# One column group for the final sum of a decode step: four shifted weight windows, one cast, one store of eight rows

## The chip, the cores and the metric

The kernel runs on one core of a Trainium2 chip. The metric is the device time of one execution in microseconds (us), the median of several runs. All times below are in us unless ns is written. The engines are named as in the profile: PE is TensorE (PEld its weight loads), DVE is VectorE, ACT is ScalarE, POOL is GpSimd, SP is SyncE, whose queue starts nearly all transfers.

## The reference

Two batch rows (`B = 2`, one token each, `D = 512`) go through an attention block with cached keys and values and, beside it, through a small dense block; a gate mixes the two results.

```python
g = sigmoid((x * gate_w).sum(-1, keepdims=True))
q = x @ wq                                  # 512 -> 32 heads x 128
p = softmax(q . k_cache / sqrt(128))        # 32 heads, 4096 cached positions, per batch row
a = (p . v_cache) @ wo                      # 4096 -> 512
b = relu(x @ w1) @ w2                       # 512 -> 1376 -> 512
out = g * a + (1 - g) * b                   # (2, 1, 512), bf16
```

The caches are 2 x 64 MB in bf16, wq and wo 4 MB each, w1 and w2 1.4 MB each. All inputs are bf16.

## The kernel before

**Order of the work.** Each engine has a list of instructions written out by hand; a small helper (`_Prog`) turns named markers into semaphore waits. SP's queue loads wq and w1, then ten pieces of the key cache and eleven of the value cache into a few regions of one SBUF tile `kv`, each as soon as its region has been read (line 286), then a part of w2 (`w2x`, line 289), wo in two parts (semaphores `wo0`, `wo1`, lines 291 and 293; wo's rows 0 to 23 and 24 to 31) and the rest of w2 in three parts of 7, 2 and 1 rows (`w2b`, `w2c`, `w2d`, line 295). Here a "row" of wo or w2 is one contraction step: 128 partitions x 512 columns. The last entry of the queue is the store of the result (line 296).

**Start.** GpSimd fills constants (lines 232 to 260), among them `ident16`, from which VectorE makes the selection matrices `selx` and `sel2` (lines 324 and 326). TensorE computes the gate, q (lines 344 and 424) and turns q by transposes (line 371); the dense block's hidden row is made, and `ffn_relu` writes it, with relu and the factor `1 - g`, into `hT` (line 406): `[128, 14, 2]`, that is 14 contraction rows of two weight columns, one for each batch row.

**Middle.** VectorE transposes key tiles (line 417), TensorE computes scores (line 445, with a second matmul on held weights, line 424, through the helper `mm_held`), then softmax, then the values in four column groups at a time (line 510). Line 537 gathers head results with fp32 matmuls into one column group.

**The tail.** After the last value piece `o_turn` (line 549) turns the attention result into `oW` (line 552): `[128, 32, 2]`, 32 contraction rows of two weight columns. The output is a sum over 32 rows of wo and 14 of w2. `project` (line 564) handles the four `w2x` rows and wo's rows 0 to 23 with matmuls of 512 columns, row r in column group r % 4, so that four partial sums stand at PSUM partitions 0, 32, 64 and 96. VectorE copies them to SBUF as `pr_sb` (line 569). `last_rows` then runs `fin_row` (line 573) for wo's rows 24 to 31, for `pr_sb` with `sel2` as weights (this adds the four partial sums), and for ten rows of w2. In `fin_row` the 512 output columns are cut into four pieces of 128; piece c is computed in column group c and lands on partitions 32c and 32c + 1:

```python
for c in range(4):
    e.matmul(psf(32 * c, 32 * c + 2, FIN_C0, 128), lhsT=lhsT, rhs=rhs[:, c * 128:(c + 1) * 128],
             tile_position=(0, 32 * c))
```

`store` casts two pieces on VectorE (line 592) and two on ScalarE (line 594) into `out_sb`, `[2, 512]`, and SP stores it as two rows of 1024 bytes.

Of the kernel before, what the change touches and what calls it, by code (L numbers as in the profile page):

```python
# [14 lines left out]
HALF = 16384  # L15
REGION = {"A": 0, "Ah": HALF, "B": 2 * HALF, "C": 4 * HALF}
WO_CUT = 24


class _Marker:  # L20
# [67 lines left out]
def bass_gated_mix__gqa_block_cached__dense_activation_relu__decode_kernel(  # L88
# [50 lines left out]
    nrow = sb("nrow", [128, 8, 4], dt.float32)  # L139
    negm = sb("negm", [128, 32], dt.float32)  # L140
    lsum = sb("lsum", [128, 2, 2], dt.float32)
    sel2 = sb("sel2", [128, 2], dt.float32)
    lrow = sb("lrow", [128, 2], dt.float32)
    rinv = sb("rinv", [32, 2], dt.float32)
    mask8 = sb("mask8", [128, 8], dt.bfloat16)
# [3 lines left out]
    sell_odd = sell[:, 1:65].rearrange("p (u f two) -> p u f two", u=8, two=2)[:, :, :, 0]  # L149
    s4 = sb("s4", [32, 4, 128], dt.bfloat16)  # L150
    O_sb = sb("O_sb", [32, 2, 128], dt.bfloat16)
    oW = sb("oW", [128, 32, 2], dt.bfloat16)
    hT = sb("hT", [128, 14, 2], dt.bfloat16)
    out_sb = sb("out_sb", [2, 512], dt.bfloat16)
    w2x = sb("w2x", [128, 4, 512], dt.bfloat16)
    hrowT = kt[:, 2, 0:448]

# [35 lines left out]
        return m  # L193


    both, lo, hi = (0, 1), (0,), (1,)
    k_pieces = [(0, both, "A"), (1, both, "B"), (2, lo, "C"), (3, both, "A"), (4, both, "B"), (2, hi, "C"),
                (5, both, "A"), (6, both, "B"), (7, lo, "C"), (7, hi, "A")]
# [21 lines left out]
    def pool(fn, waits=(), signal=None):  # L220
        P.add("pool", fn, waits=[marker(w) for w in waits], signal=marker(signal) if signal else None)
# [7 lines left out]
    def pe(fn, waits=(), signal=None, dwaits=()):  # L229
# [4 lines left out]
    pool(lambda g: g.affine_select(out=ident16[:], in_=ident16[:], pattern=[[-1, 128]],  # L234
                                   compare_op=ALU.not_equal, fill=1.0, base=0, channel_multiplier=1),
         waits=["c_i16z"], signal="c_i16")
    pool(lambda g: g.memset(xTw[:], 0.0), signal="c_xTw")
    pool(lambda g: g.memset(qbuf[:], 0.0), signal="c_qbuf")  # L238
    pool(lambda g: g.memset(mpad[:], 0.0), signal="c_mpad")
    pool(lambda g: g.memset(w2x[:], 0.0), signal="c_w2x")  # L240
    pool(lambda g: g.memset(sell[:], 0.0), signal="c_s0")  # L241
    pool(lambda g: g.memset(sell_odd, 1.0), waits=["c_s0"], signal="c_s1")
# [50 lines left out]
    sp(lambda e: e.dma_start(wreg[:, 512 * WO_CUT:HALF], wo_in[:, 512 * WO_CUT:HALF]).then_inc(sem["wo1"], 16))  # L293
    for name, r0, r1 in (("w2b", 0, 7), ("w2c", 7, 9), ("w2d", 9, 10)):
        sp(lambda e, name=name, r0=r0, r1=r1: e.dma_start(w2[:, r0:r1, :], w2_in[:, r0:r1, :]).then_inc(sem[name], 16))
    sp(lambda e: e.dma_start(out.rearrange("b s n -> (b s) n"), out_sb[:, :]).then_inc(sem["out"], 16),
       dwaits=[(sem["fin"], 4)])
    sp(lambda e: e.wait_ge(sem["out"], 16))


    def gate():
        for t in range(4):
            pe(lambda e, t=t: e.transpose(PSB[0:128, XT_B0 + 4 * t:XT_B0 + 4 * t + 3], x_sb[0:3, t::4], ident16[0:3, 0:3]),  # L303
               waits=(["c_i16"] if t == 0 else []), dwaits=([(sem["x"], 16), (sem["gw"], 16)] if t == 0 else []),
               signal=("pe_xT" if t == 3 else None))
        dve(lambda v: v.tensor_copy(out=xT3[:, :, 0:3], in_=PSB[0:128, XT_B0:XT_B0 + 16].rearrange("p (t b) -> p t b", t=4)[:, :, 0:3]),  # L306
            waits=["pe_xT"], signal="dve_xT")
        dve(lambda v: v.tensor_copy(out=xTw[:, :, 0:2], in_=xT), waits=["dve_xT", "c_xTw"], signal="dve_xTw")
        dve(lambda v: v.tensor_tensor(out=xg[:], in0=xT, in1=xT3[:, :, 2:3].to_broadcast([128, 4, 2]), op=ALU.mult),
            waits=["dve_xT"], signal="dve_xg")  # L310
        dve(lambda v: v.tensor_reduce(out=xgs[:], in_=xg[:].rearrange("p t b -> p b t"), axis=AX.X, op=ALU.add),
            waits=["dve_xg"], signal="dve_xgs")
        pe(lambda e: e.matmul(psf(0, 128, G_C0, 2), lhsT=ones32[:, :], rhs=xgs[:, :], start=True, stop=True),
           waits=["dve_xgs", "c_ones"], signal="pe_z")
        act(lambda a: a.activation(out=ez[:], in_=psf(0, 128, G_C0, 2), func=ACT.Exp, scale=-1.0),
            waits=["pe_z"], signal="act_ez")
        dve(lambda v: v.tensor_scalar(out=ez1[:], in0=ez[:], scalar1=1.0, scalar2=None, op0=ALU.add),
            waits=["act_ez"], signal="dve_ez1")
        dve(lambda v: v.reciprocal(out=gb[:], in_=ez1[:]), waits=["dve_ez1"], signal="dve_g")
        dve(lambda v: v.tensor_scalar(out=gm[:], in0=gb[:], scalar1=-1.0, scalar2=1.0, op0=ALU.mult, op1=ALU.add),  # L320
            waits=["dve_g"], signal="dve_gm")
        dve(lambda v: v.tensor_reduce(out=maskc[:], in_=ident16[:].rearrange("p (k c) -> p c k", c=4), axis=AX.X, op=ALU.add),
            waits=["c_i16"], signal="dve_maskc")
        dve(lambda v: v.tensor_reduce(out=selx[:, 24:32], in_=ident16[:].rearrange("p (t h c) -> p h t c", t=4, c=4),
                                      axis=AX.XY, op=ALU.add), waits=["c_i16", "c_selx"], signal="dve_selx")
        dve(lambda v: v.tensor_reduce(out=sel2[:], in_=ident16[:].rearrange("p (t q) -> p q t", t=4)[:, 0:2, :], axis=AX.X, op=ALU.add),
            waits=["c_i16"], signal="dve_sel2")

    def q_window(b, blk, par, u):
        h = 2 * (blk % 2) + par  # L330
# [72 lines left out]
    def ffn_relu():  # L403
        dve(lambda v: v.transpose(out=hrowT, in_=psf(0, 128, HR_C0, 448)), waits=["pe_h"], signal="dve_hrT")
        for b in range(2):
            dve(lambda v, b=b: v.tensor_scalar(out=hT[:, :, b], in0=hrowT[:, b:448:32], scalar1=0.0,
                                               scalar2=gm[:, b:b + 1], op0=ALU.max, op1=ALU.mult),
                waits=["dve_hrT", "dve_gm"], signal=f"dve_h{b + 1}")


    def k_turn(i):
# [6 lines left out]
            waits=([f"pe_sc_{i - NKT}"] if i >= NKT else ["dve_h2"] if i == 2 else []), dwaits=([landed["k", n]] if first else []),  # L418
            signal=(f"k_read_{n}" if turn_end[n] == i else f"kt_{i}"))

    def mm_held(e, out, lhsT, rhs, start, stop, size=(128, 128), at=(0, 0)):
        a = e.lower_ap(rhs)
        w = e.lower_ap(lhsT, for_matmul_weights=True)
        return e.add_instruction(mybir.InstMatmult(  # L424
            start_tensor_calc=start, stop_tensor_calc=stop, tile_size=size, tile_position=at, ldweights=False,
            name=nc.get_next_instruction_name(), engine=mybir.EngineType.PE, ins=[a, w], outs=[e.lower_ap(out)]))

    def k_scores(i):
# [118 lines left out]
    def o_turn():  # L547
        for dq in range(4):
            pe(lambda e, dq=dq: e.matmul(psf(0, 128, R_C0, 64), lhsT=s4[:, dq, :], rhs=O_sb[:, :, 32 * dq:32 * dq + 32],
                                         start=(dq == 0), stop=(dq == 3), tile_position=(0, 0)),  # L550
               waits=(["dve_O0", "dve_O1", "c_s4"] if dq == 0 else []), signal=("pe_R" if dq == 3 else None))
        dve(lambda v: v.tensor_copy(out=oW[:, :, :].rearrange("p r b -> p b r"), in_=psf(0, 128, R_C0, 64).rearrange("p (b r) -> p b r", b=2)),
            waits=["pe_R"], signal="dve_oW")

    def pr_clear():
        dve(lambda v: v.memset(psf(0, 128, PR_C0, 512), 0.0), waits=["act_exp3"], signal="dve_pr0")
# [1 line left out]
    def project(rows):  # L558
        for r in rows:
            t = r % 4  # L560
            lhsT, rhs = (hT[:, 14 + r, :], w2x[:, t, :]) if r < 0 else (oW[:, r, :], wreg[:, r * 512:(r + 1) * 512])
            dw = {-4: [(sem["w2x"], 32)], 0: [(sem["wo0"], 16)]}.get(r, [])
            waits = {-4: ["dve_h2", "dve_pr0"], 0: ["dve_oW"]}.get(r, [])
            pe(lambda e, t=t, r=r, lhsT=lhsT, rhs=rhs: e.matmul(psf(32 * t, 32 * t + 2, PR_C0, 512), lhsT=lhsT, rhs=rhs,
                                                               start=(r < 0), stop=(r >= WO_CUT - 4), tile_position=(0, 32 * t)),
               dwaits=dw, waits=waits, signal=("pe_pr" if r == WO_CUT - 1 else None))

# [1 line left out]
        dve(lambda v: v.tensor_copy(out=pr_sb, in_=psf(0, 128, PR_C0, 512)), waits=["pe_pr"], signal="dve_pr")  # L569

    def fin_row(first, last, lhsT, rhs, dw, waits, signal):
        for c in range(4):
            pe(lambda e, c=c: e.matmul(psf(32 * c, 32 * c + 2, FIN_C0, 128), lhsT=lhsT, rhs=rhs[:, c * 128:(c + 1) * 128],  # L573
                                       start=first, stop=last, tile_position=(0, 32 * c), skip_group_check=True),
               dwaits=(dw if c == 0 else []), waits=(waits if c == 0 else []), signal=(signal if c == 3 else None))

    def last_rows():
        for r in range(WO_CUT, 32):
# [1 line left out]
        fin_row(False, False, sel2[:, :], pr_sb, [], ["dve_pr", "dve_sel2"], None)  # L580
        for r in range(10):
            dw = {0: [(sem["w2b"], 16)], 7: [(sem["w2c"], 16)], 9: [(sem["w2d"], 16)]}.get(r, [])
            fin_row(False, r == 9, hT[:, r, :], w2[:, r, :], dw, [], "pe_fin" if r == 9 else None)

    def store():
        def piece(c):
            return out_sb[:, 128 * c:128 * c + 128], psf(32 * c, 32 * c + 2, FIN_C0, 128)

        for c in range(4):
            dst, src = piece(c)  # L590
            if c < 2:
                dve(lambda v, dst=dst, src=src: v.tensor_copy(out=dst, in_=src).then_inc(sem["fin"], 1), waits=["pe_fin"])
            else:
                act(lambda a, dst=dst, src=src: a.activation(out=dst, in_=src, func=ACT.Copy).then_inc(sem["fin"], 1), waits=["pe_fin"])  # L594


    gate()
# [64 lines left out]
```

## Time and profile before

| what | value |
|---|---|
| time, median of 3 runs (range) | 344.44 (344.37 to 344.48) |
| the profiled execution's own time | 344.36 |
| its span, from the first to the last instruction | 343.0 |
| mean granted TensorE clock, share of full | 0.806 |
| busy: PE / PEld / DVE / ACT / POOL | 199.7 / 52.2 / 192.9 / 15.0 / 9.5 |
| moved from memory | 145.57 MB, mean 424 GB/s |

The granted clock is the share of its pulses that TensorE's throttle lets through; the views by windows and by slices show it over time. In a view of the timeline, each line is a group of like instructions: start, time that they cover, engine, line of the kernel, operation, tile written <- tiles read, shapes, count, and in brackets the engine's idle time before it with what ended it. In the chain of waits each line is a piece of the chain of work that ended last, in order of time.

### The profile page before, as it was taken

How to read it: one execution, taken by the hardware profiler on the slowest of the kernel's cores; microseconds unless marked ns; L12 is line 12 of the kernel's file. 1: busy time of each engine (PE TensorE's matmuls, PEld its weight loads, DVE VectorE, ACT ScalarE, POOL GpSimd, SP SyncE). 2: the span in 40 equal slices, each digit the busy share in tenths (PEclk: the TensorE clock that was granted, in tenths of full speed). 3: DMA queues.
4: the chain of work that ended last, by engine and by line, in shares of the span. 5: the costliest groups of instructions: out<-in, count | busy, mean ns of one | idle time of the engine just before them, and what ended most of it. 6: DMA issues, size and time to landing. Idle time of an engine off the chain costs nothing.

```text
span 343.0 us, 2484 instructions
## 1 busy us (share of the span) xinstructions
PE 199.7 (58%) x1232; PEld 52.2 (15%) x952; DVE 192.9 (56%) x136; ACT 15.0 (4%) x54; POOL 9.5 (3%) x21
## 2 busy tenths in 40 slices
PE   0440596998797996988999274005065043143656
PEld 0110121111111111111111031002023011021312
DVE  0240896996998996989999596304016103031221
ACT  1040001010001001000000300000000000000000
POOL 8200000000000000000000000000000000000000
PEclk9995599899898999999999767558568656587656
DMA  7998989999999989999999999999999999999996
GB/s 306 470 489 367 489 367 426 432 482 413 443 428 426 485 383 466 390 417 430 428 428 478 436 407 482 405 459 407 405 428 461 420 443 436 397 434 436 419 418 243
DMA packets 4081, 145.57 MB, mean 424 GB/s; under 512 B 459, under 2 KB 592, under 8 KB 872
## 3 DMA queue, kind: packets, MB, share of 16 engines
q1 hardware_dynamic: 4066, 145.43, 98.5%
q8 instruction: 8, 0.13, 0.2%
q14 instruction: 1, 0.01, 0.0%
q10 hardware_dynamic: 6, 0.00, 0.0%
HBM read 145.43 MB, written 0.00 MB: 424 GB/s over the span
## 4 chain that ended last, share of the span: by engine, by line
DMA 65%; PE 17%; DVE 15%; ACT 1%; SPq 0%; issue 0%; DVEq 0%
DMA kv<-in_A_k_cache_dram 27%; DMA kv<-in_A_v_cache_dram 26%; DVE kt L417 12%; DMA kv<-in_B_w_dram 8%; PE PS L510 5%; PE PS L424 5%; PE PS L445 5%; DMA kv<-in_A_wq_dram 4%; PE PS L344 1%; DVE kt L492 1%; ACT kt L465 1%; DVE qrow L368 1%; DVE mpad L453 1%; DVE kt L469 0%; PE PS L371 0%
## 5 line engine op out<-in xcount | busy, mean ns | idle before, releaser
L417 DVE STREAM_TRANSPOSE kt<-kv 128x2048 f32<-128x2048 f32 x64 | 141.1, 2273 | 23.0 <-DMA kv<-in_A_k_cache_dram 23.0
L445 PE MATMUL PS<-kt,qbuf 128*128 128x512 bf16 x256 | 106.1, 414 | 32.8 <-DVE kt L417 27.8
L424 PE MATMUL PS<-kt,qbuf 128*128 128x512 bf16 x256 | 105.5, 412 | 0.0
L510 PE MATMUL PS<-kv,kt 128*32 128x512 bf16 x512 | 46.1, 534 | 90.0 <-DMA kv<-in_A_v_cache_dram 77.1
L518 DVE TENSOR_TENSOR qbuf<-PS,maskc 128x512 f32<-128x512 f32 x11 | 7.6, 692 | 95.8 <-PE PS L510 95.7
L445 PEld LDWEIGHTS PS<-kt,qbuf 128*128 128x128 bf16 x256 | 25.6, 100 | 141.7 <-DVE kt L417 72.8
L510 PEld LDWEIGHTS PS<-kv,kt 128*32 128x32 bf16 x512 | 17.7, 125 | 116.8 <-issue 74.8
L492 DVE TENSOR_TENSOR kt<-kt,mask 128x512 bf16<-128x512 bf16 (+1 forms) x17 | 19.3, 1179 | 0.0
L339 ACT ACTIVATE qbuf<-PS 32x4 bf16<-32x4 bf16 (+1 forms) x40 | 7.6, 190 | 107.9 <-PE PS L424 105.9
L521 DVE TENSOR_REDUCE qbuf<-qbuf 128x128 f32<-128x512 f32 x11 | 11.3, 1025 | 0.4
L344 PE MATMUL PS<-kv,xTw 128*32 128x512 bf16 (+1 forms) x32 | 5.3, 690 | 3.3 <-DMA kv<-in_A_wq_dram 3.3
L594 ACT ACTIVATE out_sb<-PS 2x128 bf16<-2x128 f32 x2 | 0.5, 271 | 144.6 <-PE PS L573 144.6
L537 PE MATMUL PS<-qbuf,selx 128*32 128x128 f32 x22 | 4.9, 387 | 2.0 <-DVE qbuf L521 2.0
L368 DVE CAST qrow<-PS 128x256 bf16<-128x256 f32 x2 | 2.6, 1516 | 5.5 <-PE PS L424 5.5
L465 ACT ACTIVATE kt<-PS,negm 128x512 bf16<-128x512 f32 x4 | 2.7, 686 | 58.9 <-DVE negm L461 58.9
L303 PE MATMUL PS<-ident,x_sb 3*128 3x3 bf16 x4 | 0.3, 166 | 8.1 <-POOL sell L241 8.1
L306 DVE COPY xT<-PS 128x12 bf16<-128x12 bf16 x1 | 0.2, 170 | 8.4 <-PE PS L303 8.4
L238 POOL MEMSET qbuf<- 128x5120 bf16 x1 | 4.4, 4361 | 0.0
L537 PEld LDWEIGHTS PS<-qbuf,selx 128*32 128x32 f32 x22 | 3.4, 162 | 4.6 <-DVE qbuf L521 3.2
L424 PE MATMUL PS<-kv,xTw 128*32 128x512 bf16 (+1 forms) x24 | 3.7, 511 | 0.0
L453 DVE TENSOR_REDUCE mpad<-PS 128x2 f32<-128x2048 f32 x1 | 2.3, 2291 | 2.2 <-PE PS L424 2.2
L469 DVE STREAM_TRANSPOSE kt<-kt 128x1024 bf16<-128x1024 bf16 x2 | 2.5, 1246 | 1.6 <-ACT kt L465 1.5
(67 smaller groups left out, 32.3 us busy)
## 6 DMA issues: line engine op xcount, KB each, us to landing
kv<-in_A_v_cache_dram SPq DMA_DIRECT2D x6, 4096.0 KB, 36.9
kv<-in_A_k_cache_dram SPq DMA_DIRECT2D x4, 4096.0 KB, 31.7
kv<-in_A_wq_dram SPq DMA_DIRECT2D x1, 4096.0 KB, 12.2
kv<-in_A_wo_dram SPq DMA_DIRECT2D x1, 3072.0 KB, 23.4
kv<-in_B_w_dram SPq DMA_DIRECT2D x1, 1376.0 KB, 15.1
kv<-in_A_wo_dram SPq DMA_DIRECT2D x1, 1024.0 KB, 25.5
kv<-in_B_w_dram SPq DMA_DIRECT2D x1, 896.0 KB, 27.2
kv<-in_B_w_dram SPq DMA_DIRECT2D x1, 256.0 KB, 27.4
```

The lines of the kernel that those rows point to most:

```text
L339: act(lambda a: a.activation(out=out, in_=src, func=ACT.Copy), waits=waits, signal=f"q_{b}_{u}_{blk}_{par}")
L344: return e.matmul(out, lhsT=xTw[:, t, :], rhs=rhs, start=(t == 0), stop=(t == 3), tile_position=(0, 32 * c))
L368: dve(lambda v, dst=dst, src=src: v.tensor_copy(out=dst, in_=src), waits=[f"pe_qr{half}"], signal=f"qrow{half}{e2}")
L417: dve(lambda v: v.transpose(out=dst, in_=pairs[:, h, 64 * a:64 * a + 64, :]), waits=([f"pe_sc_{i - NKT}"] if i >= NKT else ["dve_h2"] if i ...
L424: return e.add_instruction(mybir.InstMatmult(start_tensor_calc=start, stop_tensor_calc=stop, tile_size=size, tile_position=at, ldweights=F ...
L445: return e.matmul(out, lhsT=lhsT, rhs=rhs, start=start, stop=stop)
L465: act(lambda a, g=g, par=par: a.activation(out=E_sb[:, 32 * g:32 * g + 32, 16 * par:16 * par + 16], in_=psf(0, 128, (2 * par + g) * BANK, ...
L492: dve(lambda v: v.tensor_tensor(out=out, in0=src.unsqueeze(2).to_broadcast(shape), in1=mask8[:].unsqueeze(1).unsqueeze(3).to_broadcast(sha ...
L510: pe(lambda e, j=j, t=t: e.matmul(psf(32 * t, 32 * t + 32, V_BS[n % 2] * BANK, 512), lhsT=v_weights(n)[:, j], rhs=rows[:, :, j, :], start= ...
L518: dve(lambda e: e.tensor_tensor(out=parts, in0=psf(0, 128, V_BS[n % 2] * BANK, 512).rearrange("p (c d) -> p c d", c=4), in1=maskc[:].unsqu ...
L521: dve(lambda e: e.tensor_reduce(out=X2[:, b, k, :], in_=parts.rearrange("p c d -> p d c"), axis=AX.X, op=ALU.add), waits=[f"dve_m{n}"], si ...
L537: pe(lambda e, n=n, w0=w0: e.matmul(psf(0, 32, O_C0, 128), lhsT=selx[:, w0:w0 + 32], rhs=X2[:, b, n - mine[0], :], start=(n == mine[0]), s ...
```

## The change

All four pieces of 128 output columns are computed in column group 0. The weights of a row become a window of eight columns: `hT`, `oW` and `sel2` are widened from 2 to 11 columns, filled with zeros by GpSimd, and the two batch columns stand at 3 and 7 (`BOTH`). For piece k the window starts at column 3 - k, so that the two real columns stand at k and 4 + k, and the other six are zeros. The four matmuls of a row add into the same eight PSUM partitions; partition 4b + k ends up with piece k of batch row b. One cast on VectorE and one store of eight rows of 128 elements follow. For w2's last row, `held_row` loads a block of 32 weight columns ahead of the wait for `w2d`, and the first of the row's four matmuls runs on it without a load of its own; the other three are ordinary matmuls. Constants: `NB = 4`, `NG = 1`, `WIDE = 11`.

```diff
-    sel2 = sb("sel2", [128, 2], dt.float32)
+    sel2 = sb("sel2", [128, WIDE], dt.float32)
...
-    oW = sb("oW", [128, 32, 2], dt.bfloat16)
-    hT = sb("hT", [128, 14, 2], dt.bfloat16)
-    out_sb = sb("out_sb", [2, 512], dt.bfloat16)
+    oW = sb("oW", [128, 32, WIDE], dt.bfloat16)
+    hT = sb("hT", [128, 18, WIDE], dt.bfloat16)
+    out_sb = sb("out_sb", [32 * NG, 128], dt.bfloat16)
...
+    BOTH = slice(NB - 1, 2 * NB, NB)
...
+    pool(lambda g: g.memset(sel2[:], 0.0), signal="c_sel2")
     pool(lambda g: g.memset(xTw[:], 0.0), signal="c_xTw")
     pool(lambda g: g.memset(qbuf[:], 0.0), signal="c_qbuf")
     pool(lambda g: g.memset(mpad[:], 0.0), signal="c_mpad")
+    pool(lambda g: g.memset(hT[:], 0.0), signal="c_hT")
+    pool(lambda g: g.memset(oW[:], 0.0), signal="c_oW")
     pool(lambda g: g.memset(w2x[:], 0.0), signal="c_w2x")
...
-    sp(lambda e: e.dma_start(out.rearrange("b s n -> (b s) n"), out_sb[:, :]).then_inc(sem["out"], 16),
-       dwaits=[(sem["fin"], 4)])
+    sp(lambda e: e.dma_start(out.rearrange("b s (k n) -> (b s k) n", k=4), out_sb[0:8, :]).then_inc(sem["out"], 16),
+       dwaits=[(sem["fin"], 1)])
...
     def fin_row(first, last, lhsT, rhs, dw, waits, signal):
-        for c in range(4):
-            pe(lambda e, c=c: e.matmul(psf(32 * c, 32 * c + 2, FIN_C0, 128), lhsT=lhsT, rhs=rhs[:, c * 128:(c + 1) * 128],
-                                       start=first, stop=last, tile_position=(0, 32 * c), skip_group_check=True),
+        for n in range(4):
+            k, g = divmod(n, NG)
+            pe(lambda e, k=k, g=g: e.matmul(psf(32 * g, 32 * g + 2 * NB, FIN_C0, 128), lhsT=lhsT[:, NB - 1 - k:3 * NB - 1 - k],
+                                            rhs=rhs[:, (NB * g + k) * 128:(NB * g + k + 1) * 128], start=(first and k == 0),
+                                            stop=(last and k == NB - 1), tile_position=(0, 32 * g), skip_group_check=True),
...
+    def held_row(dw):
+        for g in range(NG):
+            pe(lambda e, g=g: e.ldweights(hT_cols(9 * WIDE + NB - 1), tile_position=(0, 32 * g)))
+        for n in range(4):
+            k, g = divmod(n, NG)
+
+            def fn(e, k=k, g=g):
+                out, rhs = psf(32 * g, 32 * g + 2 * NB, FIN_C0, 128), w2[:, 9, (NB * g + k) * 128:(NB * g + k + 1) * 128]
+                lhsT = hT[:, 9, NB - 1 - k:3 * NB - 1 - k]
+                if k == 0:
+                    return mm_held(e, psf(32 * g, 32 * g + 32, FIN_C0, 128), hT_cols(9 * WIDE + NB - 1), rhs, False, False, (128, 32), (0, 32 * g), True)
+                return e.matmul(out, lhsT=lhsT, rhs=rhs, start=False, stop=(k == NB - 1), tile_position=(0, 32 * g), skip_group_check=True)
+            pe(fn, dwaits=(dw if n == 0 else []), signal=("pe_fin" if n == 3 else None))
...
     def store():
-        def piece(c):
-            return out_sb[:, 128 * c:128 * c + 128], psf(32 * c, 32 * c + 2, FIN_C0, 128)
-
-        for c in range(4):
-            dst, src = piece(c)
-            if c < 2:
-                dve(lambda v, dst=dst, src=src: v.tensor_copy(out=dst, in_=src).then_inc(sem["fin"], 1), waits=["pe_fin"])
-            else:
-                act(lambda a, dst=dst, src=src: a.activation(out=dst, in_=src, func=ACT.Copy).then_inc(sem["fin"], 1), waits=["pe_fin"])
+        dve(lambda v: v.tensor_copy(out=out_sb[0:8, :], in_=psf(0, 8, FIN_C0, 128)).then_inc(sem["fin"], 1), waits=["pe_fin"])
```

The writers of `hT`, `oW` and `sel2` (lines 406, 552 and 326) and the two-column weights of `project` address the columns `BOTH`.

## The prediction

> **What bounds the kernel now.** I read the chain of waits over the last 17 us first, to see which work ends last.
>
> ```profile
> 7 pieces in order of time: start us, us, what
> 313.39 27.43 DMA kv<-in_B_w_dram
> 340.82 0.04 issue
> 340.86 0.26 PE PS L573 x4
> 341.12 0.02 issue
> 341.14 0.28 DVE out_sb L592
> 341.45 0.28 DVE out_sb L592
> ```
>
> The last load, w2's tenth row, has landed at 340.82; everything before it is streaming from memory (145 MB at 424 GB/s, by the page). Behind it stand four matmuls (0.26), two casts in a row on VectorE with two on ScalarE beside them (0.28 + 0.03 + 0.28), and the store: its issue runs from 341.76 to 342.05 and SyncE then waits 0.9, to the span's end at 343.0. The profiled execution took 344.36, so 1.36 lies outside the span; the median of the three runs is 344.44, 0.08 above it. I work from 344.36.
>
> Next the timeline of TensorE from 336.78 on, to see how much spare time it has before that landing.
>
> ```profile
> 336.78 1.07 PE L564 MATMUL PS<-kv,oW 128*2 128x512 bf16 x8
> 337.63 1.07 PE L573 MATMUL PS<-kv,oW 128*2 128x128 bf16 x32
> 338.64 0.61 PE L573 MATMUL PS<-qbuf,sel 128*2 128x128 f32 x8
> 339.70 0.95 PE L573 MATMUL PS<-kv,hT 128*2 128x128 bf16 x36 [0.44 <-DMA kv<-in_B_w_dram]
> 340.86 0.23 PE L573 MATMUL PS<-kv,hT 128*2 128x128 bf16 x4 [0.22 <-DMA kv<-in_B_w_dram]
> ```
>
> TensorE has little to do: 32 matmuls of 128 columns fit in 1.07. That works only because the four matmuls of a row stand in four column groups and run side by side. One row of four takes (1.07 - 0.31) / 7 = 0.108, where 0.31 is one matmul's duration in the groups. The trace's starts are 0.107 apart. The 28 matmuls from 339.70 take 0.56 in a narrower window, so a row there takes (0.56 - 0.22) / 6 = 0.056: the granted clock has doubled in between. The change puts all four matmuls into one group, so I looked for rows in which matmuls with weights of their own follow each other in one tile.
>
> ```profile
> 19.42 1.03 PE L371 MATMUL PS<-ident,qrow 128*128 128x128 bf16 x8 [2.73 <-DVE qrow L368]
> 262.26 2.34 PE L537 MATMUL PS<-qbuf,selx 128*32 128x128 f32 x10
> ```
>
> L371: eight bf16 matmuls of 128 columns in one tile, each with its load (0.14 each), in 1.03; one lasts 0.31, so the pitch is 0.72 / 7 = 0.103 (0.107 after the first). L537: ten fp32 passes in one column group at a pitch of (2.34 - 0.42) / 9 = 0.213; a fp32 matmul is two such passes. So one tile takes one matmul at a time, 0.107 for 128 bf16 columns at half clock, and the load hides behind the matmul before.
>
> Last the clock, by windows (us, then busy time of PE, PEld, DVE, ACT, POOL, the granted clock, DMA share, GB/s).
>
> ```profile
> 257.68:261.09 3.41, 1.12 (x24) 0.67 (x28) 2.17 (x1) 0.00 (x0) 0.00 (x0) 1.00 1.18 509
> 261.09:264.50 3.41, 3.41 (x26) 2.06 (x18) 1.72 (x2) 0.00 (x0) 0.00 (x0) 0.50 0.93 403
> 264.50:267.92 3.42, 0.10 (x1) 0.00 (x0) 2.11 (x4) 0.00 (x0) 0.00 (x0) 1.00 1.13 484
> ...
> 329.36:332.77 3.41, 2.39 (x24) 0.61 (x16) 1.36 (x2) 0.00 (x0) 0.00 (x0) 0.50 1.01 435
> 332.77:336.18 3.41, 2.08 (x18) 0.82 (x22) 0.98 (x3) 0.00 (x0) 0.00 (x0) 0.50 0.92 386
> 336.18:339.60 3.42, 3.07 (x56) 1.26 (x48) 0.69 (x1) 0.00 (x0) 0.00 (x0) 0.50 0.90 360
> 339.60:343.00 3.40, 1.07 (x40) 0.57 (x40) 0.56 (x2) 0.54 (x2) 0.00 (x0) 1.00 0.09 27
> ```
>
> The clock changes on a grid of 3.41. After a window with 2.39 busy it stays at 0.50; after one with 3.07 it is 1.00. (A window with 2.68, from 308.88, was enough too.) The window from 261.09 had 2.24 of its 3.41 in L537, one column group, and full clock followed: a single group counts as busy.
>
> **The change part by part.**
>
> *Matmuls of the tail.* The count stays: 8 rows of wo, sel2's row, 10 rows of w2, four matmuls each. All now have the tile at column 0. I count in units of 128 bf16 columns: 32 (wo) + 4 x 2 passes x 2 = 16 (fp32) + 40 (w2) = 88 units, one after another. A unit costs 0.107 at half clock and 0.056 at full clock. The start is unchanged at 337.63: line 564's 24 matmuls stay in four groups, and wo's last piece landed at 337.5. If the grid lies as in the profiled execution, the window 336.18 to 339.60 is busy throughout, and full clock comes at 339.60. Until then 1.97 / 0.107 = 18.4 units are done. The other 69.6 take 69.6 x 0.056 = 3.90, to 343.50. From the end of a stream to the release of the casts was 0.26 - 0.056, some 0.2 with both issue gaps left where they are: 0.19 taken, 343.69. Before, this point was 341.12: **+2.57**. All loads have landed by 340.86, while row 7 of w2 is not reached before 341.8; the waits for w2b, w2c, w2d and for VectorE's copy (done at 338.6) disappear in the serial stream.
>
> The grid need not lie the same in another execution: nothing in the kernel's events is aligned with it. Busy time runs without a break from 335.12, and about 0.2 before that counts, so the doubling can come anywhere from 337.3 to 340.7. With c as the time at half clock after 337.63, the stream ends at 342.56 + 0.48 c. For c = 0 this is +1.63, for c = 3.06 it is +3.09.
>
> *Last row.* Weights loaded ahead serve the first of its four matmuls; the other three load their own. The load at 340.86 was 0.08, and it hid nothing else; with TensorE 2.6 behind the landing, the gain is 0. If TensorE were in time, it would be at most 0.08.
>
> *Casts.* One cast of 8 x 128 in place of two of 2 x 128 in a row: 128 elements per partition as now (0.28). Saved: 0.31, the distance 341.14 to 341.45. ScalarE's two went beside them and give nothing.
>
> *Store.* Eight rows of 256 B for two of 1024 B. The issue is 0.285 now; the bounds are 0.23 (the one-row load of gate_w on ScalarE's queue) and 0.87 (the twelve-row load of w2x on SyncE). The landing wait of 0.9 has no nearer row. I take +0.05, nearest to the present store, with -0.05 and +0.6 as ends.
>
> *Zero fills on GpSimd.* Three are added ahead of w2x. By qbuf's 4.36 for 5120 elements, 352 + 198 + 22 elements cost some 0.5, with starts 0.7. What comes late is selx's reduction on VectorE (10.84, waiting for the last fill); VectorE's next work waits for TensorE until 16.74, so 5 us cover it. xTw's fill is 0.12 later, and its reader runs at 8.64 for a matmul at 13.08. The cost is 0; uncovered it would be 0.7. The wider pitch of hT and oW touches three small VectorE writes. hT's (0.38, at 23.98) precede the wait for K. oW's cast (0.23) ends at 334.96, and TensorE starts at 335.12 on the landing of wo: 0 to +0.1, taken 0. The two-column loads of lines 564 (0.11 each) lie under rows of 0.43.
>
> *Sum.* 344.36 + 2.57 - 0.31 + 0.05 = 346.67; with c between 0 and 3.06, the store's ends and 0.1 for oW, 345.6 to 347.8. The middle of the grid's positions (c = 1.5) gives 346.5. I give 346.6.
>
> **The rivals.**
>
> *Loads that show at full clock.* No row has bf16 matmuls with own weights in one tile at full clock. A load lasts 0.08 there (L573), longer than a matmul's 0.056. If each waits for its load, the pitch is 0.082, and the 53.6 bf16 matmuls after 339.60 cost 53.6 x 0.026 = 1.4 more: 348.0 (347.5 to 348.3 over the grid). Against it: at half clock L371's 0.14 load hides behind 0.107, and L573's loads overlap four groups at 0.056. The Trainium skill, "TensorE: Matmul & The Clock Gate", under "The mechanism", says that loads overlap matmuls in flight only if the row groups differ, which they never do here; under "Back-to-back issue gap" it gives about 81 ns per pair of 128 columns, by which I estimate 348.0 as well. The trace's L371 disagrees with that rule at half clock.
>
> *The clock stays at half.* If 8 columns of one group count for less than L537's 32, all 88 units cost 0.107: 9.42, release at 347.25, +6.13 - 0.31 + 0.05, 350.2. Against it: window 261.09, and the window from 336.18, whose matmuls have two columns in each group and still brought full clock. The skill's same page, "What's actually happening", has the doubling after about 3.4 us of busy time without regard to width; the trace's grid of 3.41 agrees.
>
> *The four matmuls overlap in one group after all.* Each window has different weights, but if the array took them as it takes four groups now, TensorE would be in time for the landing at 340.82 and the casts' 0.31 would remain: 344.1, no change that counts. It decides at 3.2 us for the 84 units before the last row, 0.038 a unit; the shortest pitch in one tile is 0.107 at half clock, which halved is 0.054. Faster than 343.97 (0.31 + 0.08 less) nothing in the change can make it.
>
> **How the numbers follow.** The serial stream with hidden loads has 0.78, visible loads 0.11, half clock 0.07, overlap 0.03, and 0.01 is left for a gain that I have no mechanism for. Range 345.5 to 348.3: the first two cases with the store's ends. The measurement tells 0.2%, 0.69 us, from no change; the first three cases are all beyond it: slower 0.96, same 0.03, faster 0.01.
>
> **What would show it.** In the changed kernel's timeline, the tail's matmuls start 0.107 and later 0.056 apart, singly, from 337.6 to about 343.5; no wait for w2d; the chain ends in TensorE, one cast of 0.28, the store. A pitch near 0.08 at clock 1.00 is the first rival; a clock of 0.50 past 341 the second; a wait for w2d at 340.8 refutes me.

## The result, and the profile after

The changed kernel takes 346.37 us (median of six runs, 345.97 to 347.14), the kernel before 344.37 (344.26 to 344.48) on the same chip: a ratio of 1.0062, 95% interval 1.0052 to 1.0072. It is slower by 2.0 us, and its six runs spread over 1.2 us where those of before spread over 0.2 (in the later comparisons, 16 to 27 runs of before spread over 0.6 to 0.9). The profiled execution took 346.99, with a span of 345.7.

The chain of waits of the changed kernel, over its last 10 us (start, duration, what):

```profile
335.58 2.73 PE PS L571 x24
338.31 5.60 PE PS L581 x76
343.91 0.06 PE PS L431
343.97 0.18 PE PS L597 x3
344.15 0.02 issue
344.18 0.28 DVE out_sb L615
```

The landing of w2's last row is gone from the chain. TensorE is on it from line 571 (`project`) through 80 matmuls (line 581 `fin_row`, 431 and 597 the last row) to the one cast. The timeline shows the same stretch by tiles, and the store:

```profile
338.09 2.94 PE L581 MATMUL PS<-kv,oW 128*8 128x128 bf16 x32
...
340.87 1.04 PE L581 MATMUL PS<-qbuf,sel 128*8 128x128 f32 x8
...
341.74 2.17 PE L581 MATMUL PS<-kv,hT 128*8 128x128 bf16 x36
...
343.75 0.22 PE L431 MATMUL PS<-kv,hT 128*32 128x128 bf16 x1
...
343.81 0.33 PE L597 MATMUL PS<-kv,hT 128*8 128x128 bf16 x3
344.18 0.28 DVE L615 CAST out_sb<-PS 8x128 bf16<-8x128 f32 x1 [5.12 <-PE PS L597]
344.48 0.32 SPq L303 DMA_DIRECT2D out_dram<-out_sb  x1
```

The 32 matmuls of wo's rows took 1.07 before and now take 2.94. No line has a wait for w2b, w2c or w2d in brackets. The 36 matmuls at full clock have a pitch of (2.17 - 0.22) / 35 = 0.056, and their weight loads last 0.087 each. This is the loads' line in the view by source (count, then the shortest, the median and the longest duration in ns, and the first and the last start):

```profile
L581 PEld LDWEIGHTS PS<-kv,hT x36: 87/87/88, 341.6 to 343.6; 128*8 128x8 bf16 x36
```

The clock, by windows on its own grid (columns as in the prediction):

```profile
336.74:340.15 3.41, 3.41 (x36) 2.41 (x29) 0.69 (x1) 0.00 (x0) 0.00 (x0) 0.50 0.80 315
340.15:343.56 3.41, 3.41 (x56) 3.25 (x54) 0.00 (x0) 0.00 (x0) 0.00 (x0) 1.00 0.01 4
```

Full clock came at 340.15, 2.06 into the single stream.

### The profile page after: what moved, and what is told of

Its sections match the earlier page's. It is cut to its first block, busy times and chain, and to the rows that moved or that the text cites. A ratio compares the mean times of both kernels' runs of the same rounds, so it can differ in the third digit from the quotient of the medians.

```text
span 345.7 us, 2484 instructions
## 1 busy us (share of the span) xinstructions
PE 202.7 (59%) x1232; PEld 56.4 (16%) x952; DVE 192.9 (56%) x135; ACT 14.5 (4%) x52; POOL 10.1 (3%) x24
## 4 chain that ended last, share of the span: by engine, by line
DMA 64%; PE 20%; DVE 15%; ACT 1%; issue 0%; SPq 0%; DVEq 0%
DMA kv<-in_A_v_cache_dram 32%; DMA kv<-in_A_k_cache_dram 27%; DVE kt L424 12%; PE PS L517 6%; PE PS L431 5%; PE PS L452 5%; DMA kv<-in_A_wq_dram 4%; PE PS L581 2%; PE PS L351 1%; ACT kt L472 1%; PE PS L571 1%; DVE qrow L375 1%; DVE mpad L460 1%; DVE kt L499 0%; DVE kt L476 0%
```

## The experiments

The theory is that of the prediction: 88 units in one column group, one after another, and the position of the clock's grid sets how long they take. The rivals are that the wide weights and fills cost the time, that the short rows of the store do, that loads show, or that the spread is that of the loads' landings.

**Wide weights, four groups** (e1). Weights, fills and wide pitch of the changed kernel, but the tail, casts and store of the kernel before.

```diff
-            pe(lambda e, k=k, g=g: e.matmul(psf(32 * g, 32 * g + 2 * NB, FIN_C0, 128), lhsT=lhsT[:, NB - 1 - k:3 * NB - 1 - k],
...
+            pe(lambda e, c=c: e.matmul(psf(32 * c, 32 * c + 2, FIN_C0, 128), lhsT=lhsT, rhs=rhs[:, c * 128:(c + 1) * 128],
+                                       start=first, stop=last, tile_position=(0, 32 * c), skip_group_check=True),
...
```

> The widened weights, the three added zero fills and the writes with the wide pitch are kept; the matmuls of the tail stand in four column groups again, with four casts and the store of two rows. Theory (the serial stream in one group is the loss): the time of before, 344.4 (344.2 to 344.6), although the cast into oW takes 0.45 as in the changed kernel, since the start of the tail has room until the landing of w2's last row. Rival (the wide weights cost it: fills, a cast into oW longer by 0.2, loads with another pitch): at least half of the loss stays, 345.4 or more.

Measured: 344.49 (344.29 to 344.69), ratio 1.0000, interval 0.9991 to 1.0009. In its timeline:

```profile
334.96 0.44 DVE L559 CAST oW<-PS 128x64 bf16<-128x64 f32 x1 [0.49 <-PE PS L556]
335.45 2.73 PE L571 MATMUL PS<-kv,oW 128*2 128x512 bf16 x24 [0.53 <-DVE oW L559]
337.97 1.07 PE L580 MATMUL PS<-kv,oW 128*2 128x128 bf16 x32
...
339.94 1.22 PE L580 MATMUL PS<-kv,hT 128*2 128x128 bf16 x40 [0.35 <-DMA kv<-in_B_w_dram]
```

The cast into oW does take 0.44, and TensorE starts 0.3 later than before, but it still waits 0.35 for w2. So the fills, the wide pitch and the longer cast cost nothing while there are four groups. Weight loads of eight columns are not part of e1, which loads two; the loss lies in the grouping, in these loads or behind them.

**Nothing held** (e4). Only the last row is put back.

```diff
-            if r == 9:
-                held_row(dw)
-            else:
-                fin_row(False, False, hT[:, r, :], w2[:, r, :], dw, [], None)
+            fin_row(False, r == 9, hT[:, r, :], w2[:, r, :], dw, [], "pe_fin" if r == 9 else None)
```

> The changed kernel with an ordinary last row of w2 (no weights held). Theory: TensorE reaches that row 2 to 3 after its landing and loads hide behind the matmul before, so no difference: 346.4, within 0.3 of the changed kernel, w2's last four matmuls 0.056 apart as the others. Rival (the held load helps): 0.1 to 0.2 longer; or the separate load costs: shorter.

Measured: 346.38 (346.05 to 347.09), ratio 1.0058, interval 1.0046 to 1.0070: no difference from the changed kernel. Its profile is also a second position of the grid. Full clock came at 338.57; the granted clock is 0.50 ahead of that and 1.00 from there on:

```profile
338.57:343.30 4.73, 4.73 (x77) 4.42 (x74) 0.38 (x1) 0.00 (x0) 0.00 (x0) 1.00 0.21 79
```

The chain of waits has

```profile
338.21 5.13 PE PS L581 x80
343.35 0.02 issue
343.37 0.28 DVE out_sb L612
```

The stream started at 337.99, 0.10 before that of the changed kernel's profile, and ended 0.80 before it. The held load gives nothing; the earlier clock gives 0.70, where 0.48 for each us of half clock (2.06 less 0.58) make 0.71.

**Full clock ahead of the tail** (e2 and e9). Matmuls that nothing reads fill TensorE's gaps ahead of the tail, so that the clock has risen by then. In e2 they are 8, 4 and 8, in e9 12, 6 and 10.

```diff
+    def filler(count):
+        for j in range(count):
+            pe(lambda e: e.matmul(psf(0, 128, 2 * BANK, 512), lhsT=ident16[:, :], rhs=kt_late[:, 0:512], start=True, stop=True))
...
             o_gather(1, range(n_first, last))
+            filler(8)
...
     project(range(-4, 0))
+    filler(4)
...
     o_turn()
+    filler(8)
     project(range(WO_CUT))
```

> The changed kernel with 20 matmuls of 512 columns added that nothing reads (8 before the last value piece, 4 after the rows of w2x, 8 before line 571), so that TensorE's windows ahead of the tail are busy. Theory: the clock is at full when the single stream starts, 88 units at 0.056 make 4.93 from the landing of wo's last piece, and all runs come to 345.7 (345.4 to 346.0) with a spread under 0.5, in place of 346.4 with a spread of 1.2. Rival (the length of the stream does not hang on the position of the clock's grid, the spread is that of the loads' landings): 346.4 and a spread near 1.2 as before.

Measured: 345.85 (345.52 to 347.05), ratio 1.0047, interval 1.0034 to 1.0060. Four of six runs lie between 345.52 and 345.92, but the spread of under 0.5 was missed: one run took 347.05 with a span of 345.8, another 346.67 with a span of 344.4, so that its excess lies outside the span. The first of the two was followed up with more filler:

> The kernel with filler again, with 12, 6 and 10 matmuls of 512 columns in place of 8, 4 and 8. In the first filler kernel's trace the clock fell to half at 328.3 and was back only at 331.7, since 8 matmuls at full clock fill 1.7 of a gap of 4.1; in another position of the grid it may not have been back in time, which would make its one long span of 345.8. Theory: with more filler the clock is full at the start of the single stream in all runs, spans 344.4 to 344.8, times 345.7 (345.4 to 346.1). Rival (the stream's length does not hang on the grid): spans up to 346 remain.

Measured: 345.67 (345.42 to 345.92), ratio 1.0033, interval 1.0020 to 1.0045. All spans lie between 344.2 and 344.6. In the timeline of e9 the stream runs at full clock from its start:

```profile
337.69 1.95 PE L581 MATMUL PS<-kv,oW 128*8 128x128 bf16 x32 [0.93 <-DMA kv<-in_A_wo_dram]
339.48 1.04 PE L581 MATMUL PS<-qbuf,sel 128*8 128x128 f32 x8
340.36 2.17 PE L581 MATMUL PS<-kv,hT 128*8 128x128 bf16 x36
```

wo's 32 matmuls take 1.95 in place of 2.94. Work that computes nothing made the changed kernel faster by about 0.7 (346.37 to 345.67; over the kernel before in the same comparison, +2.00 became +1.17) and took its spread over six runs from 1.2 to 0.5; the kernel before lies between 344.12 and 344.99 in the same comparison. That the long run of e2 was one in which the clock had fallen back is argued only, since it left no trace.

**Two groups** (e3 and e8). `NB = 2`: two column groups, two shifted windows in each, one cast over 36 partitions, two stores of four rows. In e3 both stores are on SP's queue, and group g has pieces 2g and 2g + 1; in e8 group g has pieces g and 2 + g, with one store on SP's and one on ScalarE's queue. The stores shown are those of e8.

```diff
-NB = 4
+NB = 2
...
+        for g, q in ((0, sp), (1, act)):
+            q(lambda e, g=g: e.dma_start(out.rearrange("b s (k g n) -> g (b s k) n", k=2, g=2)[g],
+                                         out_sb[32 * g:32 * g + 4, :]).then_inc(sem["out"], 16), dwaits=[(sem["fin"], 1)])
...
```

> NB = 2: two column groups with two shifted windows each, one cast over 36 partitions, two stores of four rows one after the other on SP's queue; w2's last row has its first pair held. Theory: 44 steps in place of 88. At half clock until about 340 and then at full clock, the stream ends some 0.6 after that of before (0 to 1.3 by the position of the grid); less 0.31 for the casts and 0.3 more for the second store's issue: 344.9 (344.3 to 345.7), so at least half of the loss of 2.0 goes. Rival (the loss lies in what follows the matmuls, the eight short rows of the store, or in the wide weights): 346.0 or more.

Measured: 345.67 (345.27 to 346.02), ratio 1.0033, interval 1.0021 to 1.0045: at the end of the expected range, short of half the loss. TensorE's part came as expected, the store's did not. In the timeline of e3:

```profile
340.96 0.22 PE L432 MATMUL PS<-kv,hT 128*32 128x128 bf16 x2
341.01 0.22 PE L598 MATMUL PS<-kv,hT 128*4 128x128 bf16 x2
341.27 0.28 DVE L616 CAST out_sb<-PS 36x128 bf16<-36x128 f32 x1 [2.54 <-PE PS L598]
341.59 1.39 SPq L304 DMA_DIRECT2D out_dram<-out_sb  x2
```

The cast starts 0.13 later than the first cast of before. But the two issues take 0.66 and 0.68, where one of 0.3 was expected: their rows have two strides in the result (k and b). The next pair of runs takes that away.

> NB = 2 with the pieces dealt out in turn (group g has pieces g and 2 + g), so that each group's four rows have one stride in the result; one cast over 36 partitions, one store on SP's queue, one on ScalarE's. Theory (the earlier kernel with two groups lost its 1.1 in two issues of 0.69 each, whose rows needed two strides): issues near 0.3 side by side, TensorE in time or up to 0.6 late by the position of the clock's grid: 344.5 (344.2 to 345.1). Rival (two groups are too slow, whatever the store): 345.3 or more.

Measured: 344.74 (344.58 to 345.67), ratio 1.0013, interval 1.0004 to 1.0022. The issues are 0.30 and 0.27:

```profile
341.56 0.28 DVE L616 CAST out_sb<-PS 36x128 bf16<-36x128 f32 x1 [2.76 <-PE PS L598]
341.87 0.30 SPq L305 DMA_DIRECT2D out_dram<-out_sb  x1
341.88 0.27 ACTq L305 DMA_DIRECT2D out_dram<-out_sb  x1
```

With half the units in a row, most of the loss of 2.0 is gone; 0.34 is left. In this profile TensorE is 0.4 later than before at the first cast (341.56 against 341.14), which uses up the 0.31 of the cast; SP then waits 1.1 for both landings in place of 0.9. How much of the 0.4 is the grouping is not shown, since the stream also starts 0.43 later (338.06 against 337.63), after a later landing of wo. Over all runs the median span is 343.2 against 343.0, and the median time outside the span (time less span) 1.71 against 1.40; no profile shows where the latter comes from.

**Four groups, one cast** (e5 and e6). From the kernel before: one cast over 98 partitions, two stores of four rows from partitions 32 apart, on two queues. e6 also holds the last row's weights in all four groups.

```diff
-    sp(lambda e: e.dma_start(out.rearrange("b s n -> (b s) n"), out_sb[:, :]).then_inc(sem["out"], 16),
-       dwaits=[(sem["fin"], 4)])
...
+        for b, q in ((0, sp), (1, act)):
+            q(lambda e, b=b: e.dma_start(out[b].rearrange("s (c n) -> (s c) n", c=4), out_sb[b:b + 97:32, :]).then_inc(sem["out"], 16),
+              dwaits=[(sem["fin"], 1)])
...
+        dve(lambda v: v.tensor_copy(out=out_sb[0:98, :], in_=psf(0, 98, FIN_C0, 128)).then_inc(sem["fin"], 1), waits=["pe_fin"])
```

> The kernel before, its tail in four column groups, with one cast on VectorE over 98 partitions in place of four casts, and two stores of four rows, one on SP's queue and one on ScalarE's. Theory: the tail waits for w2's last row as before, and the single cast saves its 0.31 less what the second queue's issue takes longer than SP's 0.285 (0.23 to 0.55 were seen there): 344.3 (344.1 to 344.6). Rival (the cast over partitions that hold old scores, or eight rows of 256 bytes, cost more than 0.3): 344.8 or more.

> As the kernel with four groups and one cast, with the weights of w2's last row loaded ahead in all four groups (32 columns each). Theory: the four matmuls start at the landing without their loads, which last 0.08 but overlap with the matmuls' own start: 0.00 to 0.08 less than that kernel, 344.25. Rival (held weights of 32 columns write 32 partitions and cost more): not faster or slower than that kernel by 0.1.

Measured: e5 345.12 (344.77 to 345.28), ratio 1.0019, interval 1.0010 to 1.0028; e6 344.86 (344.51 to 345.42), ratio 1.0017, interval 1.0008 to 1.0026. Both expectations failed; e5's time is in the range of its rival, though not by the cast that the rival named first. The timeline of e5:

```profile
341.31 0.29 DVE L587 CAST out_sb<-PS 98x128 bf16<-98x128 f32 x1 [2.92 <-PE PS L574]
341.63 0.61 SPq L298 DMA_DIRECT2D out_dram<-out_sb  x1
341.63 0.60 ACTq L298 DMA_DIRECT2D out_dram<-out_sb  x1
```

The cast is 0.29 as expected. The issue of four rows from partitions 32 apart takes 0.6, twice that of four neighbouring ones (e8), and SP waits 1.3 after it: +0.33 and +0.4 against the cast's -0.30. These make the +0.4 of the spans (medians 343.4 against 343.0); the rest of the 0.72 that e5 is slower lies outside the span (1.77 against 1.40), and no profile shows its cause. Nor does the profile show how much of the longer wait is the second queue and how much the source. Holding the four loads made no difference that the intervals can tell: e6's median span is 343.4 too.

**oW by columns** (e7, one round). The changed kernel with `oW` as `[128, WIDE, 32]`.

```diff
-    oW = sb("oW", [128, 32, WIDE], dt.bfloat16)
+    oW = sb("oW", [128, WIDE, 32], dt.bfloat16)
...
```

> The changed kernel with oW laid out as [128, 11, 32], so that VectorE's cast writes 32 neighbouring elements for each batch row. Theory (the cast went from 0.23 to 0.44 because each element is written 22 bytes from the last): the cast takes 0.25 or less, and the tail starts at the landing of wo, 0.1 to 0.2 earlier. Rival (the longer cast comes of the wait or of the tile's size): 0.44 stays. The time cannot tell this with a spread of 1.2; the cast's row does.

Measured: 346.43 (two runs, 345.92 and 346.94). Its timeline:

```profile
334.97 0.23 DVE L559 CAST oW<-PS 128x64 bf16<-128x64 f32 x1 [0.48 <-PE PS L556]
335.36 2.73 PE L571 MATMUL PS<-kv,oW 128*2 128x512 bf16 x24 [0.42 <-DMA kv<-in_A_wo_dram]
```

The cast is back at 0.23, and line 571 starts on the landing of wo, 0.16 after the cast's end, where in the changed kernel it started 0.06 after the cast's end. The longer cast comes of the pitch.

**Two groups of 256 columns** (e10), a last try at a version that beats both: the kernel before with two matmuls of 256 columns a row and one cast each on VectorE and ScalarE.

```diff
-        for c in range(4):
-            pe(lambda e, c=c: e.matmul(psf(32 * c, 32 * c + 2, FIN_C0, 128), lhsT=lhsT, rhs=rhs[:, c * 128:(c + 1) * 128],
+        for c in range(2):
+            pe(lambda e, c=c: e.matmul(psf(32 * c, 32 * c + 2, FIN_C0, 256), lhsT=lhsT, rhs=rhs[:, c * 256:(c + 1) * 256],
...
```

> The kernel before with its tail in two column groups of 256 columns (two matmuls a row in place of four), one cast of 2 x 256 on VectorE and one on ScalarE side by side, and the store of two rows of 1024 bytes as before. Theory: the casts take about 0.41 (between 0.28 for 128 and 0.69 for 512 columns) in place of 0.59, which saves 0.18; TensorE needs 44 units of time in place of 22 and is 0 to 0.7 late by the position of the grid: 344.4 (344.2 to 344.9), no change that counts. Rival (few and wide matmuls keep TensorE in time always): 344.2, faster by the 0.18.

Measured: 344.47 (344.09 to 345.62), ratio 1.0002, interval 0.9993 to 1.0011. The casts take 0.41 and 0.38. In its profile TensorE is on the chain, and the casts start 0.17 later than before (341.31 against 341.14), about what they save. How much of this is the grouping is not shown, since the stream starts 0.21 later (337.84 against 337.63). Over all runs the median span is 342.9 against 343.0, and the median time outside the span 1.71 against 1.50. No version beat the kernel before.

## Why the prediction was right

**The serial stream.** By the prediction its length is 4.93 + 0.48 c, with 0.19 to the release of the cast, c being the time at half clock. Five profiles test it, with the stream's start, c, and the release that follows, against the one seen (the end of TensorE's last piece in the chain). In e7 the granted clock rises at 340.25.

| kernel | start | c | by the formula | seen |
|---|---|---|---|---|
| changed | 338.09 | 2.06 | 344.20 | 344.15 |
| nothing held | 337.99 | 0.58 | 343.39 | 343.35 |
| oW by columns (e7) | 337.87 | 2.38 | 344.13 | 344.08 |
| filler (e2) | 337.72 | 0 | 342.84 | 342.79 |
| more filler (e9) | 337.69 | 0 | 342.81 | 342.77 |

All agree within 0.05, and all lie on one side, so that the 0.19 was some 0.05 too long. This is the step that carried the forecast.

**Loads at full clock.** The first rival is refuted: the pitch is 0.056 with loads of 0.087. The Trainium skill, "TensorE: Matmul & The Clock Gate", has a line under "The mechanism" by which loads overlap matmuls in flight only where the row groups differ, though the same section also lets a load into the background weight buffer be pulled ahead. The trace disagrees with that line, in one tile of 128 rows and 8 columns. The 81 ns for a pair that the Trainium skill's page gives under "Back-to-back issue gap" stand against 56 here.

The prediction took L371's pitch of 0.107 as one at half clock. The view by windows reads 1.00 for that stretch of before (19.40 to 20.50), but one matmul of 128 columns lasts 0.314 there, as in the tail at half clock (0.311) and not as at full clock (0.218), so the reading stands.

**The clock.** The second rival is refuted too: the window from 336.74 brought full clock, and most of it (from 338.09 on) ran in one group with 8 columns. As forecast, the switch lies elsewhere in other executions: 340.15, 338.57 and, in e3, 338.41. The Trainium skill's page "TensorE: Matmul & The Clock Gate" has the grid run free of the kernel ("What's actually happening"), and these three agree. In e9, where the clock is full in time, the spread falls from 1.2 to 0.5, no more than the kernel before has there.

**Overlap in one group** is refuted by the pitch and by the missing wait for w2.

**Cast, held load, fills.** The cast saved its 0.31 (one of 0.28 in place of two). The held load gave 0 (e4). The fills gave 0 (e1): selx's reduction moved from 10.84 to 11.40, far ahead of VectorE's next work.

**What was mis-sized.** The start of the stream was taken as unchanged; in the profile it is 338.09 in place of 337.63, 0.46 later. Of this, 0.36 is the last value piece, whose matmuls start at 328.08 in place of 327.72; in e1 they start at 327.95, in e2 at 327.94, so landings move by some tenths between executions. The rest is the cast into oW, costed at 0 to +0.1: it grew by 0.21, and 0.10 of it showed. In the kernel before a start later by 0.3 had room (e1); in the changed one it is on the chain. The store's +0.05 was +0.04 (0.32 in place of 0.285, the same wait of 0.9). Together, from 344.36: release +3.03, casts -0.31, store +0.04 make 347.1 against the 346.99 of the profiled run. Of the 0.13 between them (347.12 less 346.99), 0.07 lies outside the span, which the prediction left at 1.36 and which is 1.29 here.

The median of 346.37 lies 0.2 below the forecast of 346.6 although the stream started late in this profile. Where the grid lay in the other five runs left no trace, so the closeness of the two figures is in part luck; the steps above are not.

## What to carry to other kernels

Matmuls with few weight columns were cheap here while their outputs lay in different column groups: four of them took 0.107 at half clock, and in one group each took as much. Putting outputs side by side on neighbouring partitions made them serial, so compare the serial length with the time until the last landing, at half clock, before shortening what follows. TensorE, waiting for loads at the end, ran at half clock here (0.50 after windows with 2.39 and 2.08 busy of 3.41), and where on the grid the switch fell became part of the time once TensorE was on the chain: the wider spread of the runs came of it (1.2, and 0.5 with the clock full in time). What is saved behind the last matmul can be lost again in the store's issue, as in e3 and e5: look at the strides of both sides.

## What the runs showed of the hardware that was not expected

A VectorE cast of 64 elements per partition depends on the distance between written bf16 elements: 0.23 at 2 bytes (e7) and at 4 (before), 0.34 at 10 (two groups, `WIDE` 5), 0.44 at 22 (changed).

The issue of a small store depends on its strides: 0.29 for two rows (before), 0.32 for eight rows of neighbouring partitions (changed), 0.27 to 0.30 for four (e8); 0.60 to 0.61 for four rows from partitions 32 apart (e5), 0.66 and 0.68 for four rows with two strides in the result (e3).
